# Two feature tiles gated in one operation, the fifth tile's products moved up, and late weight clamps on VectorE

## The chip, the cores and the metric

The kernel runs on one core of a Trainium2 chip. The metric is the device time of one execution in microseconds (us); the kernel before was run three times (median 668.87 us, lowest 668.62, highest 670.48). A further execution was taken with the hardware profiler.

## The reference

Three steps follow one another, in fp32, for a batch of 4 sequences of 768 positions and a width of 384 (8 heads of 48).

```python
# 1. linear attention with a decaying state, per head
for t in range(S):
    cur = einsum('bhd,bhe->bhde', u * k[t], v[t])
    y[t] = einsum('bhd,bhde->bhe', r[t], state + cur)
    state = w * state + einsum('bhd,bhe->bhde', k[t], v[t])
# 2. gated mixer, d_ff = 1024
h = maximum(x @ w_in, 0)
conv = conv_w[0]*h[t-1] + conv_w[1]*h[t] + conv_w[2]*h[t+1]
x = (h * sigmoid(conv)) @ w_out
# 3. second mixer, d_ff = 1536
xn = (x - mean) / sqrt(var + 1e-6) * g_ln
out = x + maximum(xn @ w_ch1, 0) @ w_ch2
```

## The kernel before

**Products in three passes.** A product of fp32 accuracy is made of three TensorE passes: each operand is split into a rounded high part and the rest (names ending in h and l), and high x high, high x low and low x high are added in PSUM. VectorE makes the low part by a subtraction, ScalarE the high part by a copy.

**Attention** works on 24 tiles of 128 positions. Each tile runs as a generator (`attn_tile`, lines 367 to 404; for the first six tiles `light_tile`, lines 318 to 365) in steps: first the element-wise products on VectorE (the decay tables times r and k into `rk`, L373; for the first tiles also `z`, and `kks` by `decayed_k`, lines 252 to 258), then the dot products on TensorE (`dps`) with a masked copy into `aT`, then the products with the values and the state (`yps`), copied out as `xh` and `xl`. A mask selection for each of these tiles runs on POOL (L383, L335). The first four tiles run in `startup()` (lines 434 to 459), between steps of the weight preparation; the fifth is begun by the first step of `attention()` (lines 461 to 483), which then goes on in steps of its own.

**Weights** are prepared in 22 jobs (`wjob`, lines 141 to 174). A job loads a block by DMA from SP's queue, ScalarE takes magnitudes, a clamp follows (`magnitude`, lines 121 to 126), then three integer operations on VectorE, then the high part on ScalarE and the low part on VectorE. The clamp runs on VectorE for jobs 0 to 9 and on POOL for jobs 10 to 21. `wdo(n)` takes n steps of the current job; jobs 0 to 9 belong to the first mixer, jobs 10 to 21 to the second, and of these 15 to 21 are the second half of `w_ch1` and the last four blocks of `w_ch2`. The clamp of a job is issued within the job before it.

**First mixer** (`mixer1`, lines 600 to 614): 8 blocks of 384 positions, 8 feature tiles of 128 in each, 64 feature tiles in all. For each tile `moe1_up` (lines 524 to 539) makes the up-product (nine passes of 386 columns into a PSUM bank, of which there are two), ScalarE makes `h` by relu and the middle tap, VectorE two taps of the convolution (L535). Then `gate` (lines 513 to 516) takes the sigmoid on ScalarE and the product h x gate on VectorE (L516), and `gate_split` (lines 518 to 522) makes high and low part (L521, L522). Both are called for the tile before, while the present one is convolved. `queue_down` puts the tile's down-product (nine passes of 384 columns) into a queue, and `pump(2)` lets all but two of the queue go, so tile f's down-product is issued behind the up-product of tile f + 3. Between tiles, `after1` (lines 834 to 848) takes attention steps: one per tile in the first two blocks, 0.8 later, and weight steps.

**Second mixer** (`mixer2`): 6 blocks of 512 positions, 12 feature tiles each, with relu alone between the up-product and the down-product, queued likewise with `pump(3)`. `prefetch` and `norm` load and normalise the next block's rows meanwhile, with one small power operation per tile on POOL (L572).

**Order.** Operations called through `pe`, `vo`, `ao`, `so` and `go` keep the order in which the program issues them on their engine. Those called through `nc.vector`, `nc.scalar` and `nc.gpsimd` (`v_`, `a_`, `g_`) are placed by a planner when the program is built; `inputs(n)` and `ordered(n)` choose between the two by tile. Helper calls through the ordered engines stand in the profile under line 76.

Of the kernel before, what the change touches and what calls it, by code (L numbers as in the profile page):

```python
# [8 lines left out]
F32 = mybir.dt.float32  # L9
F32R = mybir.dt.float32r  # L10
I32 = mybir.dt.int32
AF = mybir.ActivationFunctionType
ALU = mybir.AluOpType
# [7 lines left out]
NF1 = FF1 // 128  # L21
NF2 = FF2 // 128
C = 128
TPB = S // C
NT = B * TPB
T = 384
TT = T // C
# [8 lines left out]
LAG = 3  # L36
# [13 lines left out]
def body(ctx, tc, r, k, v, w, u, w_in, conv_w, w_out, g_ln, w_ch1, w_ch2, rkT, krv, small, out):  # L50
# [6 lines left out]
    mp = ctx.enter_context(tc.tile_pool(name="mp", bufs=2))  # L57
# [6 lines left out]
    v_ = nc.vector  # L64
# [14 lines left out]
    vo = InOrder(nc.vector)  # L79
    ao = InOrder(nc.scalar)  # L80
    so = InOrder(nc.sync)
    go = InOrder(nc.gpsimd)
# [11 lines left out]
    gl = smallt[:, 3 * NP:]  # L94
# [12 lines left out]
    woh = big.tile([128, NF1, DM], F32R, name="woh")  # L107
    wol = big.tile([128, NF1, DM], F32R, name="wol")
# [12 lines left out]
    def magnitude(st, n, engine=go):  # L121

        t = ap.tile([128, WN], F32, tag="wd", name="wdec", bufs=2)[:, 0:n]
        ao.activation(out=t, in_=words(st, n)[1].bitcast(F32), func=AF.Abs)
        engine.tensor_scalar(out=t, in0=t, scalar1=W_MIN, scalar2=W_MAX, op0=ALU.max, op1=ALU.min)
        return t
# [14 lines left out]
    def wjob(src, n, hi, lo, scale=None):  # L141

        st, mag = [], []

        def load():
            st.append(io.tile([128, 2 * WN], I32, tag="st" if me >= 4 else "first", name="st", bufs=3 if me >= 4 else 4))
            dst = st[0][:, 0:2 * n]
            if len(src.shape) == 3:
                dst = dst.rearrange("p (a n) -> p a n", a=src.shape[1])
            so.dma_start(out=dst, in_=src.bitcast(I32))  # L150

        def ahead():
            if not mag:
                mag.append(magnitude(st[0], n, vo if me < 10 else go))

        def steps():
            ahead()
            t = mag[0]
            yield from decode(st[0], n, t)
            if me + 1 < min(len(wjobs), w_loaded[0]):  # L160
                wjobs[me + 1][2]()
            if len(src.shape) == 3:
                t = t.rearrange("p (a n) -> p a n", a=src.shape[1])
            kw = {} if scale is None else {"scale": gl[:, scale:scale + 1]}
            ao.activation(out=hi, in_=t, func=AF.Copy, **kw)
            yield
            if scale is None:
                vo.tensor_tensor(out=lo, in0=t, in1=hi.bitcast(F32), op=ALU.subtract)
            else:
                vo.scalar_tensor_tensor(out=lo, in0=t, scalar=kw["scale"], in1=hi.bitcast(F32),  # L170
                                        op0=ALU.mult, op1=ALU.subtract)
        me = len(wjobs)
        wjobs.append((load, steps(), ahead))
        return len(wjobs) - 1

# [34 lines left out]
    def wdo(count=1, last=None):  # L210

        for _ in range(count):
            while w_done[0] < (len(wjobs) if last is None else last + 1):
                wload(w_done[0] + 3)
                if next(wjobs[w_done[0]][1], "end") != "end":
                    break
                w_done[0] += 1
# [34 lines left out]
    def decayed_k(n):  # L252

        if n < LIGHT:
            vo.tensor_tensor(out=kks[:, n % 2, 0, :, 0:D], in0=loaded[n][1], in1=tku[:, 0], op=ALU.mult)
            return
        inputs(n).tensor_tensor(out=kks[:, n % 2, :, :, 0:D], in0=loaded[n][1].unsqueeze(1).to_broadcast([128, 2, H, D]), in1=tku,
                         op=ALU.mult)
# [175 lines left out]
    def startup():  # L434

        tiles = {n: attn_tile(n) for n in range(EARLY + 1)}

        def on(n):
            next(tiles[n], None)

        decayed = decayed_k
        on(0), decayed(0), on(0)
        on(1), state_sum(0), state_update(0), decayed(1), on(1), state_sum(1)
        wdo(1)
        on(0), on(2), state_update(1), decayed(2)
        wdo(2)
        on(2), state_sum(2), on(0)
        wdo(1)
        on(1), on(3), state_update(2), decayed(3)
        wdo(2)  # L450
        on(3), state_sum(3), on(1)
        wdo(2)
        on(2), state_update(3)
        wdo(3)
        on(2), on(3)
        wdo(1)
        on(3)
        wdo(4)
        return tiles

    def attention(tiles):

        def go_on(n):
            if 0 <= n < NT:
                next(tiles.setdefault(n, attn_tile(n)), None)

        n = EARLY
        go_on(n)
        decayed_k(n)
        yield  # L470
        load_tile(n + 2)
        decayed_k(n + 1)
        go_on(n)
        yield
        for n in range(EARLY, NT):
            state_sum(n)
            state_update(n)
            go_on(n - 1)
            go_on(n + 1)
            yield  # L480
            go_on(n)
            go_on(n + 1)
            yield
# [18 lines left out]
    def down(acc, gh, gl_, wh, wl, f, nf):  # L502
        for t in range(len(acc)):
            sl = slice(t * 128, t * 128 + 128)
            for q, (a, x) in enumerate(((gh, wh), (gh, wl), (gl_, wh))):
                pe.matmul(acc[t], lhsT=a[:, sl], rhs=x, start=(f == 0 and q == 0),
                          stop=(f == nf - 1 and q == 2))
# [5 lines left out]
    def gate(st):  # L513

        a_.activation(out=st["c"], in_=st["c"], func=AF.Sigmoid)
        v_.tensor_tensor(out=st["c"], in0=st["h"][:, 1:T + 1], in1=st["c"], op=ALU.mult)  # L516

    def gate_split(st):
        st["gh"] = mp.tile([128, T], F32R, tag="gh", name="gh", bufs=LAG + 1)
        st["gl"] = mp.tile([128, T], F32R, tag="gl", name="gl", bufs=LAG + 1)  # L520
        a_.activation(out=st["gh"], in_=st["c"], func=AF.Copy)  # L521
        v_.tensor_tensor(out=st["gl"], in0=st["c"], in1=st["gh"].bitcast(F32), op=ALU.subtract)  # L522

    def moe1_up(x, f, prev):
        ps = ps_m.tile([128, 512], F32, tag="m", name="psm")
        mm3(ps[:, 0:T + 2], [wih[:, kt] for kt in range(KT)], [wil[:, kt] for kt in range(KT)], x[0], x[1], slice(f * 128, f * 128 + 128), slice(0, T + 2))
        if prev is not None:
            gate(prev)
        st = {}
        h = st["h"] = mp.tile([128, T + 2], F32, tag="h", name="h", bufs=3)  # L530
        c = st["c"] = mp.tile([128, T], F32, tag="c", name="c", bufs=3)
        a_.activation(out=h, in_=ps[:, 0:T + 2], func=AF.Relu)
        a_.activation(out=c, in_=h[:, 1:T + 1], func=AF.Copy, scale=cw[:, 1, f:f + 1])  # L533
        for tap, o in ((0, 0), (2, 2)):
            v_.scalar_tensor_tensor(out=c, in0=h[:, o:o + T], scalar=cw[:, tap, f:f + 1], in1=c,  # L535
                                    op0=ALU.mult, op1=ALU.add)
        if prev is not None:
            gate_split(prev)
        return st

    def moe2_up(xn, f, cols):
        ps = ps_m.tile([128, 512], F32, tag="m", name="psm")
# [44 lines left out]
    def pump(n):  # L587
        while len(downq) > n:
            downq.pop(0)()

    def queue_down(st, hold, f, nf, wh, wl, then, tiles=TT):
        def go():
            if f == 0:
                hold.extend(new_acc(tiles))
            down(hold, st["gh"], st["gl"], wh(f), wl(f), f, nf)
            if f == nf - 1:
                then(hold)
        downq.append(go)

    def mixer1(x, then, before=lambda f: None, after=lambda f: None):  # L600
        hold, prev = [], None
        for f in range(NF1):
            before(f)
            st = moe1_up(x, f, prev)
            if prev is not None:
                queue_down(prev, hold, f - 1, NF1, lambda f: woh[:, f, :], lambda f: wol[:, f, :], then)
            prev = st
            after(f)
            pump(LAG - 1)
            after(f)  # L610
        before(NF1)
        gate(prev)
        gate_split(prev)
        queue_down(prev, hold, NF1 - 1, NF1, lambda f: woh[:, f, :], lambda f: wol[:, f, :], then)

    def mixer2(xn, tiles, then, before=lambda f: None, after=lambda f: None):
        hold = []
        for f in range(NF2):
            before(f)
            queue_down(moe2_up(xn, f, tiles * C), hold, f, NF2, lambda f: c2h[f // 2][:, f % 2, :],  # L620
                       lambda f: c2l[f // 2][:, f % 2, :], then, tiles)
            pump(LAG)
            after(f)
# [231 lines left out]
    for j in range(NB2):  # L855
# [11 lines left out]
        x1s, xn = normed.pop(j)  # L867
# [74 lines left out]
```

## Time and profile before

| | |
|---|---|
| median of 3 runs | 668.87 us |
| profiled execution | 670.22 us |
| its span (first to last instruction) | 668.4 us |
| mean granted TensorE clock | 0.973 of full speed |
| first up-product of the first mixer | 39.7 us |
| first up-product of the second mixer | 345.9 us |

Times within the profile are in us from the span's start, and durations of single instructions in us or ns. PE is TensorE, PEld its weight load, DVE VectorE, ACT ScalarE, SP the engine that issues the DMAs. Square brackets at the end of a row hold how long the engine stood idle before the instruction and what ended it; where the engine named there had long been done, it was another. The granted clock is a share of 2.4 GHz. Instructions of one engine overlap, so the time from one start to the next can be shorter than a duration.

### The profile page before, as it was taken

How to read it: one execution, taken by the hardware profiler on the slowest of the kernel's cores; microseconds unless marked ns; L12 is line 12 of the kernel's file. 1: busy time of each engine (PE TensorE's matmuls, PEld its weight loads, DVE VectorE, ACT ScalarE, POOL GpSimd, SP SyncE). 2: the span in 40 equal slices, each digit the busy share in tenths (PEclk: the TensorE clock that was granted, in tenths of full speed). 3: DMA queues.
4: the chain of work that ended last, by engine and by line, in shares of the span. 5: the costliest groups of instructions: out<-in, count | busy, mean ns of one | idle time of the engine just before them, and what ended most of it. 6: DMA issues, size and time to landing. Idle time of an engine off the chain costs nothing.

```text
span 668.4 us, 11712 instructions
## 1 busy us (share of the span) xinstructions
PE 633.3 (95%) x4803; PEld 573.2 (86%) x4803; DVE 437.4 (65%) x793; ACT 261.9 (39%) x514; POOL 122.5 (18%) x126
## 2 busy tenths in 40 slices
PE   9948898999998898999999999999999999999996
PEld 5747888989987897899998789999999899999995
DVE  7979999999999999878777953413422422422211
ACT  3455555465655655566764421211221111221110
POOL 6301621330332214112003620100100100100000
PEclk9876898999999999999999999999999999999999
DMA  8916434435262533102205302002001100200101
GB/s 268 313 49 209 144 106 151 135 100 185 71 215 68 173 114 115 37 1 84 71 13 177 95 0 89 8 0 86 10 0 48 49 0 29 67 0 7 42 0 52
DMA packets 25295, 56.51 MB, mean 85 GB/s; under 512 B 2961, under 2 KB 15378, under 8 KB 25234
## 3 DMA queue, kind: packets, MB, share of 16 engines
q1 hardware_dynamic: 25234, 55.68, 26.2%
q8 instruction: 40, 0.66, 0.4%
q14 instruction: 21, 0.17, 0.1%
HBM read 46.24 MB, written 9.44 MB: 83 GB/s over the span
## 4 chain that ended last, share of the span: by engine, by line
PE 50%; DVE 36%; ACT 4%; issue 4%; DMA 3%; POOL 1%; SPq 0%; DVEq 0%; ACTq 0%
PE acc L76 24%; PE psm L76 24%; DVE c L535 8%; DVE wdec L76 6%; DVE aT L389 3%; DVE c L516 3%; DVE gl L522 3%; DVE rk L373 2%; DMA x1b<-x_dram 1%; DVE rk L76 1%; DVE a L380 1%; DVE xl L398 1%; PE pxt L76 1%; DVE av L378 1%; DMA rk<-in_rkT_dram 1%
## 5 line engine op out<-in xcount | busy, mean ns | idle before, releaser
L549 DVE SCALAR_TENSOR_TENSOR rl<-psm,rh 128x512 fp32r<-128x512 f32 x72 | 49.6, 689 | 135.1 <-ACT rh L548 131.6
L548 ACT ACTIVATE rh<-psm 128x512 fp32r<-128x512 f32 x72 | 43.0, 597 | 196.1 <-PE psm L76 195.9
L76 PE MATMUL acc<-c2l,rh 128*128 128x384 f32 x288 | 97.2, 338 | 0.4 <-DVE c2l L76 0.4
L76 PE MATMUL acc<-c2h,rh 128*128 128x384 f32 x288 | 97.1, 337 | 0.0
L76 PE MATMUL acc<-c2h,rl 128*128 128x384 f32 x288 | 97.1, 337 | 0.0
L535 DVE SCALAR_TENSOR_TENSOR c<-h,tables,c 128x384 f32<-128x384 f32 x128 | 89.9, 704 | 7.0 <-ACT c L533 6.4
L76 PE MATMUL psm<-xnh,c1h 128*128 128x512 f32 x216 | 87.2, 404 | 0.8 <-ACT c1h L76 0.8
L76 PE MATMUL psm<-xnh,c1l 128*128 128x512 f32 x216 | 85.3, 395 | 0.3 <-DVE c1l L76 0.3
L76 PE MATMUL psm<-xnl,c1h 128*128 128x512 f32 x216 | 85.5, 396 | 0.0
L76 PE MATMUL psm<-xh,wih 128*128 128x386 f32 x192 | 71.3, 371 | 13.4 <-DVE xl L76 4.4
L76 PE MATMUL psm<-xl,wih 128*128 128x386 f32 x192 | 67.7, 353 | 0.0
L76 PE MATMUL psm<-xh,wil 128*128 128x386 f32 x192 | 67.7, 352 | 0.0
L76 PE MATMUL acc<-woh,gh 128*128 128x384 f32 x192 | 66.5, 347 | 0.0
L76 PE MATMUL acc<-woh,gl 128*128 128x384 f32 x192 | 65.0, 339 | 0.1
L76 PE MATMUL acc<-wol,gh 128*128 128x384 f32 x192 | 65.0, 339 | 0.0
L76 PEld LDWEIGHTS acc<-c2l,rh 128*128 128x128 f32 x288 | 54.1, 188 | 3.6 <-DVE c2l L76 0.8
L76 PEld LDWEIGHTS acc<-c2h,rh 128*128 128x128 f32 x288 | 54.1, 188 | 3.2
L76 POOL TENSOR_SCALAR wdec<-wdec 128x768 f32<-128x768 f32 (+1 forms) x13 | 40.1, 3085 | 86.4 <-ACT wdec L76 86.4
L76 PEld LDWEIGHTS acc<-c2h,rl 128*128 128x128 f32 x288 | 54.1, 188 | 0.0
L572 POOL TENSOR_TENSOR rs<-rs,nhalf 128x1 f32<-128x1 f32 x24 | 16.4, 691 | 199.4 <-DVE rs L571 198.9
L76 PEld LDWEIGHTS psm<-xh,wih 128*128 128x128 f32 x192 | 38.1, 199 | 17.0 <-ACT woh L76 4.6
L521 ACT ACTIVATE gh<-c 128x384 fp32r<-128x384 f32 x64 | 33.5, 523 | 47.2 <-DVE c L516 46.7
(133 smaller groups left out, 1142.3 us busy)
## 6 DMA issues: line engine op xcount, KB each, us to landing
rk<-in_rkT_dram SPq DMA_DIRECT2D x24, 448.0 KB, 4.4
st<-in_moe_w_ch_dram SPq DMA_DIRECT2D x12, 768.0 KB, 6.0
rv<-in_krv_dram SPq DMA_DIRECT2D x18, 448.0 KB, 4.8
kt<-in_krv_dram SPq DMA_DIRECT2D x24, 192.0 KB, 4.3
x_dram<-x SPq DMA_DIRECT2D x24, 192.0 KB, 2.1
x1b<-x_dram SPq DMA_DIRECT2D x24, 192.0 KB, 3.1
out_dram<-x1b SPq DMA_DIRECT2D x24, 192.0 KB, 1.9
st<-in_moe_w_in_dram SPq DMA_DIRECT2D x6, 512.0 KB, 9.2
```

The lines of the kernel that those rows point to most:

```text
L76: return lambda *args, **kw: tc.keep_in_program_order(op(*args, **kw))
L373: inputs(n).tensor_tensor(out=rk, in0=rk, in1=trk, op=ALU.mult)
L378: v_.tensor_tensor(out=av, in0=kks[:, n % 2, 1, :, 0:D], in1=rt, op=ALU.mult)
L380: v_.tensor_reduce(out=a8.rearrange("x (q p) o -> x q (p o)", q=2), in_=av.rearrange("x (p q) d -> x q p d", q=2), axis=AX.X, op=ALU.add)
L389: v_.copy_predicated(out=aT[:, q], mask=later.bitcast(I32).unsqueeze(1).to_broadcast([128, NP, C]), data=dps[q])
L516: v_.tensor_tensor(out=st["c"], in0=st["h"][:, 1:T + 1], in1=st["c"], op=ALU.mult)
L521: a_.activation(out=st["gh"], in_=st["c"], func=AF.Copy)
L522: v_.tensor_tensor(out=st["gl"], in0=st["c"], in1=st["gh"].bitcast(F32), op=ALU.subtract)
L535: v_.scalar_tensor_tensor(out=c, in0=h[:, o:o + T], scalar=cw[:, tap, f:f + 1], in1=c, op0=ALU.mult, op1=ALU.add)
L548: a_.activation(out=gh[:, 0:cols], in_=ps[:, 0:cols], func=AF.Relu)
L549: v_.scalar_tensor_tensor(out=gl_[:, 0:cols], in0=ps[:, 0:cols], scalar=0.0, in1=gh[:, 0:cols].bitcast(F32), op0=ALU.max, op1=ALU.subtract)
L572: g_.tensor_tensor(out=rs[:, 1:2], in0=rs[:, 0:1], in1=nhalf, op=ALU.pow)
```

## The change

`gate` and `gate_split` take a pair of feature tiles: the buffers `h`, `c`, `gh` and `gl` hold two tiles, the convolution still goes tile by tile, and the sigmoid, the product, the high part and the low part are one operation each of 2 x 384 columns. A pair is gated while the next pair's first tile is convolved, and both of its down-products are queued then. `pump` leaves three of the queue after an even tile and two after an odd one. The buffers `gh` and `gl` number three pairs where there were four tiles. In `startup()` the fifth tile's first step and its `decayed_k` come ahead of the last three weight steps, and the step of `attention()` that held them is gone. The clamps of jobs 15 to 21 run on VectorE.

```diff
--- before.py
+++ after.py
@@ -151,7 +151,7 @@
 
         def ahead():
             if not mag:
-                mag.append(magnitude(st[0], n, vo if me < 10 else go))
+                mag.append(magnitude(st[0], n, vo if me < 10 or me >= 15 else go))
 
         def steps():
             ahead()
@@ -455,7 +455,9 @@
         on(2), on(3)
         wdo(1)
         on(3)
-        wdo(4)
+        wdo(1)
+        on(4), decayed(4)
+        wdo(3)
         return tiles
 
     def attention(tiles):
@@ -465,9 +467,6 @@
                 next(tiles.setdefault(n, attn_tile(n)), None)
 
         n = EARLY
-        go_on(n)
-        decayed_k(n)
-        yield
         load_tile(n + 2)
         decayed_k(n + 1)
         go_on(n)
@@ -513,22 +512,23 @@
     def gate(st):
 
         a_.activation(out=st["c"], in_=st["c"], func=AF.Sigmoid)
-        v_.tensor_tensor(out=st["c"], in0=st["h"][:, 1:T + 1], in1=st["c"], op=ALU.mult)
+        v_.tensor_tensor(out=st["c"], in0=st["h"][:, :, 1:T + 1], in1=st["c"], op=ALU.mult)
 
     def gate_split(st):
-        st["gh"] = mp.tile([128, T], F32R, tag="gh", name="gh", bufs=LAG + 1)
-        st["gl"] = mp.tile([128, T], F32R, tag="gl", name="gl", bufs=LAG + 1)
+        st["gh"] = mp.tile([128, 2, T], F32R, tag="gh", name="gh", bufs=3)
+        st["gl"] = mp.tile([128, 2, T], F32R, tag="gl", name="gl", bufs=3)
         a_.activation(out=st["gh"], in_=st["c"], func=AF.Copy)
         v_.tensor_tensor(out=st["gl"], in0=st["c"], in1=st["gh"].bitcast(F32), op=ALU.subtract)
 
-    def moe1_up(x, f, prev):
+    def moe1_up(x, f, st, prev):
         ps = ps_m.tile([128, 512], F32, tag="m", name="psm")
         mm3(ps[:, 0:T + 2], [wih[:, kt] for kt in range(KT)], [wil[:, kt] for kt in range(KT)], x[0], x[1], slice(f * 128, f * 128 + 128), slice(0, T + 2))
         if prev is not None:
             gate(prev)
-        st = {}
-        h = st["h"] = mp.tile([128, T + 2], F32, tag="h", name="h", bufs=3)
-        c = st["c"] = mp.tile([128, T], F32, tag="c", name="c", bufs=3)
+        if not st:
+            st["h"] = mp.tile([128, 2, T + 2], F32, tag="h", name="h", bufs=3)
+            st["c"] = mp.tile([128, 2, T], F32, tag="c", name="c", bufs=3)
+        h, c = st["h"][:, f % 2], st["c"][:, f % 2]
         a_.activation(out=h, in_=ps[:, 0:T + 2], func=AF.Relu)
         a_.activation(out=c, in_=h[:, 1:T + 1], func=AF.Copy, scale=cw[:, 1, f:f + 1])
         for tap, o in ((0, 0), (2, 2)):
@@ -536,7 +536,6 @@
                                     op0=ALU.mult, op1=ALU.add)
         if prev is not None:
             gate_split(prev)
-        return st
 
     def moe2_up(xn, f, cols):
         ps = ps_m.tile([128, 512], F32, tag="m", name="psm")
@@ -588,36 +587,45 @@
         while len(downq) > n:
             downq.pop(0)()
 
-    def queue_down(st, hold, f, nf, wh, wl, then, tiles=TT):
+    def queue_down(gh, gl_, hold, f, nf, wh, wl, then, tiles=TT):
         def go():
             if f == 0:
                 hold.extend(new_acc(tiles))
-            down(hold, st["gh"], st["gl"], wh(f), wl(f), f, nf)
+            down(hold, gh, gl_, wh(f), wl(f), f, nf)
             if f == nf - 1:
                 then(hold)
         downq.append(go)
 
     def mixer1(x, then, before=lambda f: None, after=lambda f: None):
-        hold, prev = [], None
+        hold, prev, st = [], None, None
+
+        def queue(f):
+            for q in range(2):
+                queue_down(prev["gh"][:, q], prev["gl"][:, q], hold, f + q, NF1, lambda f: woh[:, f, :],
+                           lambda f: wol[:, f, :], then)
+
         for f in range(NF1):
             before(f)
-            st = moe1_up(x, f, prev)
-            if prev is not None:
-                queue_down(prev, hold, f - 1, NF1, lambda f: woh[:, f, :], lambda f: wol[:, f, :], then)
-            prev = st
+            if f % 2 == 0:
+                prev, st = st, {}
+            moe1_up(x, f, st, prev if f % 2 == 0 else None)
+            if f % 2 == 0 and f:
+                queue(f - 2)
             after(f)
-            pump(LAG - 1)
+            pump(4-1 - f % 2)
             after(f)
         before(NF1)
+        prev = st
         gate(prev)
         gate_split(prev)
-        queue_down(prev, hold, NF1 - 1, NF1, lambda f: woh[:, f, :], lambda f: wol[:, f, :], then)
+        queue(NF1 - 2)
 
     def mixer2(xn, tiles, then, before=lambda f: None, after=lambda f: None):
         hold = []
         for f in range(NF2):
             before(f)
-            queue_down(moe2_up(xn, f, tiles * C), hold, f, NF2, lambda f: c2h[f // 2][:, f % 2, :],
+            st = moe2_up(xn, f, tiles * C)
+            queue_down(st["gh"], st["gl"], hold, f, NF2, lambda f: c2h[f // 2][:, f % 2, :],
                        lambda f: c2l[f // 2][:, f % 2, :], then, tiles)
             pump(LAG)
             after(f)
```

## Rows read from the trace of the kernel before

**Rows 1.** Page, first part: busy time of each engine, share of the span, instructions.

```profile
PE 633.3 (95%) x4803; PEld 573.2 (86%) x4803; DVE 437.4 (65%) x793; ACT 261.9 (39%) x514; POOL 122.5 (18%) x126
```

**Rows 2.** Busy time by stretch: us; busy us (instructions) per engine; TensorE clock; DMA.

```profile
39.60:60.00 20.40, 13.15 (x63) 12.23 (x63) 17.38 (x34) 10.45 (x19) 3.35 (x4) 0.58 0.31 93
60.00:94.10 34.10, 30.64 (x330) 28.14 (x328) 34.03 (x51) 20.56 (x40) 15.09 (x6) 0.92 0.58 179
94.10:257.00 162.90, 156.14 (x1732) 143.32 (x1730) 159.98 (x262) 89.95 (x187) 41.73 (x37) 0.99 0.40 127
257.00:291.60 34.60, 31.77 (x326) 29.20 (x319) 30.18 (x53) 18.77 (x41) 6.88 (x7) 1.00 0.22 73
291.60:345.90 54.30, 54.25 (x358) 53.34 (x357) 43.19 (x89) 38.34 (x81) 6.79 (x5) 1.00 0.16 52
360.00:386.00 26.00, 24.51 (x126) 21.26 (x125) 22.50 (x42) 10.92 (x17) 14.39 (x9) 1.00 0.39 129
386.00:660.60 274.60, 274.60 (x1399) 248.34 (x1398) 84.16 (x170) 47.47 (x82) 12.05 (x17) 1.00 0.08 27
```

**Rows 3.** Chain that ended last: shares, then start and length of two late pieces.

```profile
PE 50%; DVE 36%; ACT 4%; issue 4%; DMA 3%; POOL 1%; SPq 0%; DVEq 0%; ACTq 0%
...
321.05 1.56 PE acc L76 x9
322.62 1.59 PE psm L76 x9
```

**Rows 4.** Groups of VectorE, 94 to 257 us: count, busy us, mean ns.

```profile
L535 DVE SCALAR_TENSOR_TENSOR c<-h,tables,c 128x384 f32<-128x384 f32 x65 | 48.2, 743 | 1.3 <-ACT c L533 1.0
L522 DVE TENSOR_TENSOR gl<-c,gh 128x384 fp32r<-128x384 f32 x33 | 19.7, 598 | 0.1
...
L516 DVE TENSOR_TENSOR c<-h,c 128x384 f32<-128x384 f32 x33 | 19.0, 576 | 0.9 <-ACT c L515 0.6
```

**Rows 5.** Timeline of VectorE, 195 to 216 us: start, length, instruction.

```profile
207.66 0.95 DVE L257 TENSOR_TENSOR kks<-kt,tables 128x768 f32<-128x768 f32 x1
208.53 0.55 DVE L516 TENSOR_TENSOR c<-h,c 128x384 f32<-128x384 f32 x1
209.00 0.55 DVE L378 TENSOR_TENSOR av<-kks,rv 128x384 f32<-128x384 f32 x1
...
210.64 1.44 DVE L522 TENSOR_TENSOR gl<-c,gh 128x384 fp32r<-128x384 f32 x1
```

**Rows 6.** Timeline of all engines, 36 to 64 us.

```profile
44.01 0.69 DVE L76 TENSOR_TENSOR wil<-wdec,wih 128x512 fp32r<-128x512 f32 x1 [1.26 <-ACT wih L76]
...
51.19 1.22 DVE L76 TENSOR_TENSOR rk<-rk,tables 112x1024 f32<-112x1024 f32 x1
...
52.51 2.08 PE L76 MATMUL dps<-rk 48*128 48x128 f32 x16 [7.16 <-ACT wih L76]
...
53.32 0.69 DVE L76 TENSOR_TENSOR z<-rk 112x512 f32<-112x512 f32 x1
53.92 0.55 DVE L76 TENSOR_TENSOR kks<-kt,tables 128x384 f32<-128x384 f32 x1
```

**Rows 7.** Clamps: on POOL, 290 to 420 us (min/median/max ns); on VectorE, whole span.

```profile
L76 POOL TENSOR_SCALAR wdec<-wdec x7: 2779/3059/3539, 294.1 to 385.0; 128x768 f32<-128x768 f32 x7
...
L76 DVE TENSOR_SCALAR wdec<-wdec 128x768 f32<-128x768 f32 x4 | 2.7, 665 | 1.3 <-ACT wdec L76 1.3
```

**Rows 8.** Timeline of TensorE, 371 to 380 us.

```profile
372.21 0.50 PE L76 MATMUL psm<-xnh,c1h 128*128 128x512 f32 x1 [0.78 <-ACT c1h L76]
...
373.26 0.50 PE L76 MATMUL psm<-xnh,c1l 128*128 128x512 f32 x1 [0.33 <-DVE c1l L76]
...
378.87 0.44 PE L76 MATMUL acc<-c2l,rh 128*128 128x384 f32 x1 [0.38 <-DVE c2l L76]
```

**Rows 9.** Timeline of POOL, one mask selection.

```profile
210.33 1.35 POOL L383 TENSOR_SCALAR_AFFINE_SELECT aT<-a 128x1024 f32<-128x1024 f32 x1 [8.15 <-DVE a L380]
```

**Rows 10.** Timeline of TensorE, 262 to 266 us.

```profile
264.31 0.44 PE L76 MATMUL psm<-xh,wih 128*128 128x386 f32 x1 [2.38 <-DVE xl L398]
```

## The prediction

> **What bounds the kernel now.** I began with the page's first part [rows 1]: TensorE is busy for 95% of the span, VectorE for 65%. That average hides two stages, so the next view was busy time by stretch [rows 2]. From 60 to 257 us VectorE has no free time (34.03 of 34.10 us, then 159.98 of 162.90), while TensorE leaves 3.46 and 6.76 us. From 291.6 us on TensorE is full (54.25 of 54.30, at the end 274.60 of 274.60) and VectorE has room (43.19 of 54.30, later 84.16 of 274.60). In the first stretch, 39.6 to 60 us, neither is full: VectorE has 3.02 us free, and TensorE stands idle for a third of it and runs at a granted clock of 0.58. In 360 to 386 us TensorE loses 1.49 us again. The chain of waits agrees [rows 3]: half of it is TensorE, 36% VectorE, and in the late stage it runs from nine down-products (1.56 us) to nine up-products (1.59 us) and back without a gap. So the kernel is first a sum of VectorE work, up to the end of attention, and then a sum of TensorE work. A saving on VectorE counts only in the first part; work that is pushed from the first part into the second is paid on TensorE.
>
> The profiled execution took 670.22 us for a span of 668.4. The three runs shown have a median of 668.87, so it lies 1.35 us above it, inside their spread. The terms below are differences; I take them off the median.
>
> **Part 1, gating two feature tiles at once.** Per pair, two products (L516) and two subtractions (L522) of 384 columns become one each of 768, on VectorE; on ScalarE two sigmoids and two copies likewise become one each. What VectorE saves depends on how a saved instruction counts. Their durations are 576 and 598 ns [rows 4]; a two-input operation of 768 columns takes 0.95 us [rows 5]. By durations a pair saves 2 x 0.576 - 0.95 + 2 x 0.598 - 0.95 = 0.45 us. But instructions overlap: in [rows 5] the 768-column one at 207.66 is followed by L516 at 208.53 and that by the next at 209.00, so in a full queue they cost 0.87 and 0.47 us, and a pair saves 2 x (0.94 - 0.87) = 0.14 us. VectorE's queue is full where the saving counts, so I take 0.14. Attention ends with about 46 of the 64 feature tiles done, hence 23 pairs: -3.2 us. Bounds: -10.3 (23 x 0.45) and 0 (the freed time becomes idle time). The new access pattern, two rows of 384 with a step, costs nothing extra as far as rows go: the 0.95 us operation also walks more than one dimension.
>
> The Trainium skill, page "VectorE: DVE Perf Modes", section "The TRN2 errata — SBUF-src ops pay a fixed extra latency per instruction", gives fp32 two-tensor operations as (N + 151) / 0.96 ns, a fixed part of 157 ns. The durations of 0.55 and 0.95 us agree with that. By it 46 saved instructions would give an estimated 7.2 us in place of 3.2, and the sum would be 660.9; the start-to-start times in [rows 5] speak for less than half of that.
>
> On ScalarE the pair's operations save time too, but it is busy for 89.95 of 162.90 us in the VectorE stage [rows 2]: nothing, and its cover would have to shrink by nearly half before it counted.
>
> The change also adds a wait: the sigmoid of an even tile now waits for the odd tile's convolution. Behind it on ScalarE stand the next relu copies, for which TensorE waits when both up-product banks are full. The sigmoid of the last tile already waited for that same convolution; it is the first half that is delayed, so I cost the wait at nothing. Every down-product comes one place later in TensorE's order (part 2), so the pair's first tile has as much cover as before and its second tile one up-product and one down-product more.
>
> **Part 2, down-products one place later.** The queue now holds tile 0's down-product until tile 4 has been multiplied, where it was tile 3. Until VectorE stops being the bound that hides in TensorE's free time; at the switch one more down-product is left for the stage in which TensorE is full, 1.56 us [rows 3]. Bounds 0 (if TensorE has the time at the switch) and 1.56; I take it whole, since [rows 2] shows 54.25 of 54.30 there.
>
> **Part 3, the fifth tile moved up.** Its three operations, rk 1.22, z 0.69 and kks 0.55 us, now run at 51 to 54 us [rows 6]; the change puts them about 41 us, ahead of the last three weight steps of the start-up. Their DMAs were issued long before, with the tables. VectorE's work stays the same; what can shrink is its idle time of 3.02 us. Its largest piece is the 1.26 us before wil at 44.01 [rows 6], a wait for a ScalarE copy: 2.46 us of tile work ahead of it should cover that. TensorE's 7.16 us gap before the dot products at 52.51 should go as well, but there VectorE sets the pace. Against it, the 16 dot products (2.08 us) and the 8 small ones that follow now stand ahead of the second up-product, so its convolution comes later. I take -1.5 us, the 1.26 and a little of the rest; bounds -3.0 and +1.5 (2.08 and about as much again, less the 2.46 us that cover it).
>
> All later attention steps come one step earlier, with their loads: the seventh tile's three transfers pass one weight load on SP's queue, which is fetched two jobs ahead, at no cost; on POOL the mask selections only come earlier. At 0.8 step per feature tile, attention ends 1.25 tiles sooner, and so 1.25 tiles more lie in the TensorE stage. Each costs 3.15 us there [rows 3] and takes 2 x 0.743 + 0.576 + 0.598 = 2.66 us out of the VectorE stage [rows 4]: 1.25 x 0.49 = +0.6 us.
>
> **Part 4, late clamps on VectorE.** Jobs 15 to 21 leave POOL: seven of 3.06 us (median) from 294 us on, against 665 ns on VectorE [rows 7]. VectorE has 3.50 us free in 360 to 386 us [rows 2] and gets 3.3 to 4.7 us in all from 294 to 390, so that is hidden; if it were not, the free time's shortfall, about 1 us, would be paid. Each weight's serial chain becomes 2.4 us shorter, and TensorE's waits for weights are 0.78, 0.33 and 0.38 us [rows 8], together the 1.49 us of [rows 2]. They should go: -1.5 us; bounds -1.5 and +1.0.
>
> **Sum.** -3.2 + 1.56 - 1.5 + 0.6 - 1.5 = -4.0 us: 664.9 us.
>
> **Rivals.**
> (a) Durations count, not starts: where VectorE's results are waited for in turn (ScalarE waits for L516 and L522's neighbours), the whole latency of a saved operation goes. Then part 1 is -10.3 and the time 657.8. For it: a VectorE operation behind POOL's mask selection is stretched to 1.44 us [rows 5], its partner being the selection at 210.33 [rows 9], and fewer operations meet fewer of those. Against it: the starts.
> (b) The saving doesn't reach the end: TensorE takes its products in order and at feature tile borders waits for attention (2.38 us for xl at 264.31 [rows 10]); if that wait, not VectorE's sum, sets the pace, part 1 gives nothing and VectorE merely idles. -0.7 us: 668.2.
> (c) Slower: the longer operation stands in front of xl or the masked products. A 768-column product ahead of them takes 0.95 us where it was 0.55, and TensorE waits in order. With 0.40 us more at each of the 18 tiles after the start-up ones that is 7.2 us, and the sum turns to +3.2: 672.1. It decides once VectorE has nothing else to do in that wait, that is, from idle time on VectorE of more than about 4 us beyond the 2.92 of 94.1 to 257 us [rows 2]. For it: waits like [rows 10]. Against it: VectorE is full there, so work does not run out. The Trainium skill, "Perfetto Trace Analysis", section "Optimizing Scalar/DVE Operations", speaks that way: where VectorE isn't saturated but causes bubbles elsewhere, breaking instructions up may finish work sooner. This trace has it saturated up to 257 us.
>
> **How the numbers follow.** Likeliest case 0.53, with its own range of 661 to 668; (a) 0.15, (b) 0.18, (c) 0.14. The range of 659 to 670.5 takes in the bounds of parts 3 and 4 and case (b), and leaves out the far end of (a) and most of (c), some 0.2. A measurement here can tell about 0.3% (2.0 us) from no change, so faster means under 666.9 and slower over 670.9. Faster: most of the likeliest case (0.45), (a) and a little of (b): 0.64. Slower: most of (c) and a bit of the likeliest case's upper end: 0.14. Same: 0.22.
>
> **What would show it.** Right: L516 and L522 with half the instructions at about 0.95 us; VectorE still full from 60 us to the end of attention, and that end 4 to 6 us sooner; TensorE's gap near 45 to 52 us mostly gone; POOL without clamps after about 260 us and no TensorE waits for c1h, c1l, c2l. Wrong: VectorE with clear idle time between 94 and 257 us (b, c), longer TensorE waits for xl or aT (c), a second up-product so late that the first stretch is not shorter (part 3), or new waits at the rl operations of 360 to 386 us (part 4).

## The result and the profile after

**Time.** 675.67 us, the median of 4 runs (674.13 to 676.2), against 669.23 for the kernel before beside it (4 runs): a ratio of 1.009, 95% interval 1.0067 to 1.0113. Slower, where I forecast 664.9, and outside the range. The profiled execution has a span of 674.1 us; before it was 668.4.

The profile page's busy line and its chain:

```profile
PE 634.4 (94%) x4803; PEld 575.8 (85%) x4803; DVE 434.1 (64%) x736; ACT 253.8 (38%) x450; POOL 88.5 (13%) x119
...
PE 62%; DVE 25%; issue 3%; ACT 3%; DMA 1%; POOL 0%; DVEq 0%; ACTq 0%
```

Against [rows 1] VectorE has 57 instructions less and 3.3 us less work, POOL 34 us less, TensorE the same number of products. The chain has moved from VectorE (36% in [rows 3], now 25%) to TensorE (50%, now 62%): the stage that TensorE bounds has grown. Busy time by stretch, columns as in [rows 2]:

```profile
39.60:60.00 20.40, 17.81 (x153) 15.81 (x153) 17.60 (x36) 11.78 (x22) 2.29 (x4) 0.67 0.43 133
60.00:94.10 34.10, 21.27 (x187) 19.84 (x191) 28.58 (x39) 15.28 (x27) 10.37 (x6) 0.71 0.50 155
94.10:257.00 162.90, 154.57 (x1702) 141.19 (x1694) 158.93 (x230) 84.84 (x157) 35.14 (x35) 1.00 0.41 127
...
291.60:345.90 54.30, 54.30 (x359) 53.70 (x358) 40.88 (x71) 35.41 (x61) 3.77 (x4) 1.00 0.16 52
...
360.00:386.00 26.00, 26.00 (x135) 23.48 (x134) 24.27 (x51) 12.55 (x19) 3.37 (x4) 1.00 0.51 172
```

The second stretch stands out: from 60 to 94.1 us TensorE does 187 instructions where it did 330, and VectorE, which had no free time there, has 5.5 us. In the last row TensorE is full from 360 to 386 us, so the waits that part 4 was after are gone. TensorE's timeline from 55 to 98 us, the rows with a wait and the up-product behind the longest one, says what stops TensorE:

```profile
60.55 0.69 PE L76 MATMUL psm<-xh,wih 128*128 128x386 f32 x1 [1.83 <-ACT aT L334]
...
83.11 2.08 PE L76 MATMUL dps<-rk 48*128 48x128 f32 x16 [12.28 <-DVE rk L76]
85.12 0.69 PE L76 MATMUL psm<-xh,wih 128*128 128x386 f32 x1
...
95.43 1.16 PE L76 MATMUL dps<-rk 48*128 48x128 f32 x16 [1.02 <-ACT h L532]
```

TensorE stands still for 12.28 us, called the hole from here on, until the product `rk` of the seventh tile is there. The up-product at 85.12 is the sixth. In the kernel before, the sixth up-product came ahead of the same dot products, which had no wait:

```profile
76.41 0.34 PE L76 MATMUL psm<-xh,wih 128*128 128x386 f32 x1
...
82.22 1.16 PE L76 MATMUL dps<-rk 48*128 48x128 f32 x16
```

VectorE's timeline of the hole and what follows it, in the changed kernel:

```profile
76.34 0.95 DVE L76 TENSOR_TENSOR kks<-kt,tables 128x768 f32<-128x768 f32 x1
77.21 0.95 DVE L76 TENSOR_TENSOR wol<-wdec,woh 128x768 fp32r<-128x768 f32 x1
...
79.48 0.95 DVE L76 SCALAR_TENSOR_TENSOR wdec<-st,wdec 128x768 int32<-128x768 int32 x1
...
80.81 1.11 DVE L76 SCALAR_TENSOR_TENSOR wdec<-st,wdec 128x768 int32<-128x768 int32 x1
81.84 1.21 DVE L76 TENSOR_TENSOR rk<-rk,tables 112x1024 f32<-112x1024 f32 x1
82.98 0.95 DVE L76 TENSOR_TENSOR wol<-wdec,woh 128x768 fp32r<-128x768 f32 x1
85.29 1.34 DVE L389 COPY_PREDICATED aT<-tables,dps 128x512 f32<-128x512 int32 x2 [1.37 <-PE dps L76]
89.64 1.23 DVE L373 TENSOR_TENSOR rk<-rk,tables 112x1024 f32<-112x1024 f32 x1 [3.01 <-DMA rk<-in_rkT_dram]
...
92.97 0.96 DVE L515 TENSOR_TENSOR c<-h,c 128x768 f32<-128x768 f32 x1 [0.91 <-ACT c L514]
```

That `rk` stands behind all but the last of the first mixer's weight steps. When they are done VectorE itself runs dry: the next convolutions belong to up-products that stand behind the dot products in TensorE's order. From the first up-product to the ninth it is idle for 8.4 us; before it was 3.1. Before, the same `rk` came ahead of the last weight job's steps, in VectorE's timeline of the kernel before:

```profile
74.31 1.23 DVE L76 TENSOR_TENSOR rk<-rk,tables 112x1024 f32<-112x1024 f32 x1
75.44 0.96 DVE L76 SCALAR_TENSOR_TENSOR wdec<-st,wdec 128x768 int32<-128x768 int32 x1
...
81.60 0.95 DVE L76 TENSOR_TENSOR wol<-wdec,woh 128x768 fp32r<-128x768 f32 x1
```

The chain that ended last, the kernel after, 40 to 120 us (start, length, piece), adds the load that comes next:

```profile
79.56 0.87 DVE wdec L76
80.89 1.03 DVE wdec L76
81.92 1.15 DVE rk L76
83.11 2.13 PE dps L76 x16
85.26 4.29 DMA rk<-in_rkT_dram
89.64 1.23 DVE rk L373
```

SP issues this load at 85.26, just when the late dot products have ended, and VectorE waits for it: 3.01 us of its idle time.

**The end of attention.** The last `xl` of attention, in the kernel before and then after (VectorE's L398 from 285 to 310 us: min/median/max ns, first and last start):

```profile
L398 DVE TENSOR_TENSOR xl<-yps,xh x2: 554/555/556, 287.5 to 297.7; 128x384 fp32r<-128x384 f32 x2
```

```profile
L398 DVE TENSOR_TENSOR xl<-yps,xh x2: 553/556/558, 287.2 to 298.3; 128x384 fp32r<-128x384 f32 x2
```

Attention ends no sooner, at 298.8 us with the operation's length against 298.3. The prediction's signs named an end 4 to 6 us sooner, and its own terms add up to 8.0 us. But fewer feature tiles are done by then: in the trace 14.0 up-products and 17.9 down-products follow it before, 16.0 and 20.1 after. From there TensorE is full, so all of it is paid. The table cuts each profiled execution at the first up-product, at the ninth (slot 8), the 41st (slot 40), the end of the last `xl`, and the first up-product of the second mixer. Its last columns hold VectorE's idle time in the three stretches from the first up-product to the last `xl`, and its busy time in all three:

```
kernel     first up  slot 8  slot 40  last xl  mixer 2  span  | mixer 2 - xl  to end | VectorE idle to slot 8, to 40, to xl | busy
before         39.7    94.1    252.1    298.3    345.9  668.4 |         47.6   322.5 |  3.1  2.9  5.5 | 247.2
after          40.3   100.5    259.9    298.8    351.4  674.1 |         52.6   322.7 |  8.4  3.9  6.2 | 240.1
```

### The profile page after: what moved, and what is told of

Read it like the earlier page. It is cut to its first block, busy times and chain, and to the rows that moved or that the text cites. A ratio compares the mean times of both kernels' runs of the same rounds, so it can differ in the third digit from the quotient of the medians.

```text
span 674.1 us, 11573 instructions
## 1 busy us (share of the span) xinstructions
PE 634.4 (94%) x4803; PEld 575.8 (85%) x4803; DVE 434.1 (64%) x736; ACT 253.8 (38%) x450; POOL 88.5 (13%) x119
## 4 chain that ended last, share of the span: by engine, by line
PE 62%; DVE 25%; issue 3%; ACT 3%; DMA 1%; POOL 0%; DVEq 0%; ACTq 0%
PE psm L76 30%; PE acc L76 29%; DVE c L535 7%; DVE wdec L76 3%; DVE aT L389 3%; DVE rk L373 2%; DVE gl L521 2%; DVE c L515 2%; PE yps L76 2%; DMA rk<-in_rkT_dram 1%; PE pxt L76 1%; ACT c L514 1%; DVE a L380 1%; DVE av L378 1%; DVE kks L257 1%
## 5 line engine op out<-in xcount | busy, mean ns | idle before, releaser
L76 PEld LDWEIGHTS psm<-xnh,c1l 128*128 128x128 f32 x216 | 40.5, 188 | 9.5
L532 ACT ACTIVATE h<-psm 128x386 f32<-128x386 f32 x64 | 31.2, 488 | 44.2 <-PE psm L76 43.7
```

What stands on the lines that cost most here:

```text
L76: return lambda *args, **kw: tc.keep_in_program_order(op(*args, **kw))
```

## The experiments

All are given as edits of the kernel before or after, with the ratio to the kernel before beside them. Each kernel has one profile, and single numbers of the table at the end of this section are read to about 1 us: the first up-product, which stands ahead of most of what the edits touch, lies between 39.0 and 41.0 us in it.

**First set: each part alone, and the change without part 3.** 668.57 us for the kernel before.

Late clamps alone (before):

```
-    mag.append(magnitude(st[0], n, vo if me < 10 else go))
+    mag.append(magnitude(st[0], n, vo if me < 10 or me >= 15 else go))
```

> The kernel before with the late clamps on VectorE alone. If they do what the prediction said, TensorE's 1.49 us of waits in the second mixer's first half block go and the time falls by 1 to 2 us (ratio 0.997 to 0.9985). If the waits are only replaced by others, no change (0.999 to 1.001).

The move alone (before):

```
-        wdo(4)
+        wdo(1)
+        on(4), decayed(4)
+        wdo(3)
...
-        go_on(n)
-        decayed_k(n)
-        yield
```

> The kernel before with the fifth tile's products moved up alone. Theory A (the earlier attention steps put the seventh tile's rk product behind the last weight steps on VectorE while TensorE's order has its dot products ahead of the next up-product): a TensorE gap of 8 to 13 us between 65 and 90 us, and a ratio of 1.006 to 1.012. Theory B (the pairs are the cause): no such gap, ratio 0.995 to 1.000.

The pairs alone, with their later down-products: the change without the two edits above.

> The kernel before with the gating in pairs alone (down-products one place later). Theory A: ratio 0.995 to 1.001, the start-up as before. Theory B: most of the loss is here, ratio 1.005 to 1.010, with VectorE idle in the first block while the pair waits for its second tile.

The change without the move:

> The changed kernel without the moved-up tile: pairs and late clamps. Theory A: ratio 0.993 to 0.999, and the gap between 65 and 90 us gone. Theory B: 1.003 to 1.008.

Measured: clamps 666.28, ratio 0.9954 [0.9933, 0.9975]; the move **675.61, 1.0093 [1.0059, 1.0127]**; pairs 666.8, 0.9965 [0.9945, 0.9985]; pairs and clamps without the move 666.47, 0.995 [0.9927, 0.9972]. The move by itself costs what the whole change costs. The clamps gain more than the 1 to 2 us expected. TensorE's waits, first of the kernel with the move alone, then of the change without it:

```profile
PE dps L76 <- DVE rk L76: 17.0, 3, 14.7
```

```profile
PE dps L76 <- ACT wih L76: 6.9, 1, 6.9
```

With the move the wait for `rk` is there without pairs and without clamps; without the move it is not, and the older gap of [rows 6] stays. The pairs and the clamps are gains, but they do not add up: both remove the second mixer's waits for weights [rows 8], the pairs by leaving one more down-product to be multiplied ahead of them.

**Second set: which piece of the move, and is the hole the cause?** 669.59 us for the kernel before.

The fifth tile moved up in the start-up, all later attention steps left where they were (after):

```
         n = EARLY
+        yield
         load_tile(n + 2)
```

> The changed kernel with an empty first attention step, so that the fifth tile's first products are moved up but no later step comes earlier. If the earlier later steps are what costs (theory A), the gap between 65 and 90 us goes and the ratio is 0.992 to 0.998. If moving the fifth tile's products ahead of the weight steps costs by itself (theory C: weights late, or the second up-product late), the ratio stays at 1.003 to 1.009.

Down-products one place earlier (after):

```
-            pump(4-1 - f % 2)
+            pump(2 - f % 2)
```

> The changed kernel with the down-products one place earlier (two of the queue left after an even tile, one after an odd one), as in the kernel before. If the later down-products feed the gap (TensorE has one less of them before the seventh tile's dot products) and cost 1.56 us at the switch, the time falls by 1.5 to 4 us against the changed kernel (ratio 1.003 to 1.007). If they cost nothing: 1.008 to 1.010; if the pair then comes late, longer waits for gl and more than 1.010.

The seventh tile's `rk` placed by the planner, so that it need not stand behind the weight steps (after):

```
-        inputs(n).tensor_tensor(out=rk, in0=rk, in1=trk, op=ALU.mult)
+        (nc.vector if n == 6 else inputs(n)).tensor_tensor(out=rk, in0=rk, in1=trk, op=ALU.mult)
```

> The changed kernel with one edit: the seventh tile's rk product alone no longer keeps the program's order on VectorE. Theory A with its place in VectorE's queue as the cause: the product runs before 75 us, the 12.28 us gap of TensorE shrinks to under 4 us and the time falls by 4 to 8 us (ratio 0.997 to 1.003). If the gap is only a symptom of VectorE's total work: the gap moves to another place and the ratio stays at 1.006 to 1.010.

Three weight steps per feature tile of the first block, where there were four (after):

```
-                wdo(2, wo_job[NF1 - 1])
+                wdo(1 + slot[0] % 2, wo_job[NF1 - 1])
```

> The changed kernel with three weight steps per feature tile in the first block where there were four, so that the rk product of the seventh tile stands ahead of one weight job more on VectorE. Theory A: gap halved or better, ratio 1.000 to 1.006. If the weights were what the first block waits for: no gain, ratio 1.008 or more.

Measured: without the shift 669.14, 0.9988 [0.9959, 1.0016]; earlier down-products 682.19, 1.0182 [1.0134, 1.023]; free `rk` 675.57, 1.0083 [1.0056, 1.011]; slower weights 671.48, 1.0028 [1.0007, 1.0048].

The shift of the steps is most of the loss: it makes the difference between 0.9988 and 1.009. That 0.9988 lies between the two cases set down, so it leaves open whether the moved first products cost something too. The free `rk` contradicts the simple form of my theory, that this one product's place in VectorE's queue makes the hole. VectorE's row, and TensorE's last wait of the block, in that kernel:

```profile
52.33 1.22 DVE L373 TENSOR_TENSOR rk<-rk,tables 112x1024 f32<-112x1024 f32 x1 [3.44 <-DMA rk<-in_rkT_dram]
```

```profile
89.41 1.09 PE L76 MATMUL pst<-rv,kks 128*64 128x48 f32 x16 [13.04 <-issue]
```

```profile
88.60 1.33 DVE L389 COPY_PREDICATED aT<-tables,dps 128x512 f32<-128x512 int32 x2
```

`rk` runs at 52 us and a hole is there all the same, 13.04 us, one step of the tile further on: its `aT` copies, VectorE's row at 88.60, stand behind the weight steps just as `rk` did. The profile names no releaser for that wait; that it ends with the first of the two copies is my reading. VectorE's idle time in the block stays at 8.4 us, but 3.44 of them are new, the wait for this `rk`'s own load in the row at 52.33. So the run shows that this one operation isn't enough, and not what a free `rk` with its data in time would give. Slower weights let VectorE reach the tile sooner, and the wait shrinks:

```profile
75.62 2.08 PE L76 MATMUL dps<-rk 48*128 48x128 f32 x16 [7.04 <-DVE rk L76]
```

VectorE's idle time in the block falls to 3.2 us and the time by 0.6%, with the shift kept. It does not fall to that of the kernel before. The earlier down-products I had wrong: I thought them a cheap 1.5 us, but the pairs need the cover, as TensorE's waits in that kernel show:

```profile
PE acc L76 <- DVE gl L521: 13.7, 12, 2.5
```

VectorE's idle time between slots 8 and 40 is 12.5 us there against 3.9.

**Third set: hole or lead?** 669.9 us for the kernel before. The shift does two things: it puts the seventh tile early (the hole), and it keeps attention a step ahead to the end (the lead). An empty step in the loop gives the lead back at one point (after, with 5 and with 8):

```
         for n in range(EARLY, NT):
+            if n == 5:
+                yield
```

> The changed kernel with an empty attention step ahead of the step that starts the seventh tile: the fifth and sixth tile stay early, the seventh and all later ones stand where they stood before. If the early seventh tile is the cause (TensorE's order has its dot products before the sixth up-product), the 12 us gap goes and the ratio is 0.994 to 1.000. If the cause is the earlier fifth and sixth tile, 1.005 to 1.009.

> The changed kernel with the empty step only ahead of the step that starts the tenth tile (three tiles later). If the early seventh tile is the cause: the gap between 65 and 90 us stays, ratio 1.006 to 1.011. If the cause is that attention ends sooner and leaves more work to TensorE's stage, the loss goes: 0.997 to 1.003.

And the slower weights without the shift, on the change without the move and on the clamps alone, to see whether slower weights are a gain by themselves:

> Pairs and late clamps without the moved tile, and three weight steps per feature tile in the first block where there were four. If VectorE's order in the first block still costs there, another 1 to 3 us: ratio 0.990 to 0.994. If VectorE's sum sets the pace, no change against pairs and clamps: 0.994 to 0.997.

> The kernel before with the late clamps on VectorE and three weight steps per feature tile in the first block. The same two cases: 0.990 to 0.994, or as the clamps alone, 0.994 to 0.998.

Measured: back from the seventh tile 668.56, 0.9979 [0.9959, 0.9998]; from the tenth 670.28, 1.0002 [0.9981, 1.0023]; slower weights 666.89, 0.9956 [0.9938, 0.9975], and 667.39, 0.9952 [0.9932, 0.9971]. TensorE's wait for the seventh tile, first with the lead given back there, then from the tenth on:

```profile
77.71 2.08 PE L76 MATMUL dps<-rk 48*128 48x128 f32 x16 [3.39 <-DVE rk L76]
```

```profile
82.61 2.08 PE L76 MATMUL dps<-rk 48*128 48x128 f32 x16 [13.67 <-DVE rk L76]
```

The second of them is the surprise: the hole is as large as in the changed kernel, and yet the time is that of the kernel before. So a hole with the lead given back costs little (0.2%, and the two intervals overlap), and keeping the lead costs 0.9% more. Slower weights gain nothing where there is no hole (0.9956 against 0.995, 0.9952 against 0.9954): they help only where the move is.

```
kernel             first up  slot 8  slot 40  last xl  mixer 2  span  | mixer 2 - xl  to end | VectorE idle to slot 8, to 40, to xl | busy
clamps alone           39.4    93.8    251.8    297.5    344.9  663.3 |         47.4   318.4 |  3.1  2.6  5.5 | 247.0
the same, slower w.    39.5    94.6    252.6    298.5    345.8  663.9 |         47.4   318.1 |  3.4  2.7  5.5 | 247.4
pairs alone            40.4    95.3    249.8    297.6    344.6  666.1 |         47.0   321.5 |  2.5  4.1  7.6 | 243.0
pairs and clamps       39.3    94.4    249.3    296.4    344.0  665.1 |         47.6   321.1 |  2.7  4.4  7.1 | 243.0
the same, slower w.    39.0    95.3    249.9    295.5    343.2  664.3 |         47.7   321.1 |  4.1  4.1  5.6 | 242.7
move alone             40.6   102.3    264.2    303.4    355.0  673.4 |         51.6   318.4 |  8.1  5.4  5.1 | 244.2
no shift               41.0    96.9    251.7    298.8    346.5  667.7 |         47.7   321.2 |  5.9  4.5  7.0 | 240.5
lead back at 7th       40.6    95.4    251.7    298.8    346.5  667.0 |         47.7   320.5 |  4.8  5.8  7.0 | 240.6
lead back at 10th      40.1   100.0    254.6    300.2    347.9  668.4 |         47.7   320.5 |  8.3  5.1  5.6 | 241.0
after                  40.3   100.5    259.9    298.8    351.4  674.1 |         52.6   322.7 |  8.4  3.9  6.2 | 240.1
after, slower w.       39.0    96.4    255.4    294.2    346.8  668.7 |         52.6   321.9 |  3.2  4.0  6.1 | 241.9
```

The column "mixer 2 - xl" separates the two: in this table it is 51.6 to 52.6 us wherever the lead is kept, and 47.0 to 47.7 wherever it is not. The lead costs TensorE's stage 4 to 5 us. It should be earned back by less work for VectorE up to the last `xl`, and so by an earlier last `xl`. VectorE's columns, with the lead less without it, show what became of that:

```
with the lead    without it                    work left out   busy   idle   last xl
move alone       before                                  2.7   -3.0   +7.1      +5.1
after            pairs and clamps                        3.9   -2.9   +4.3      +2.4
after            no shift                                3.9   -0.4   +1.1       0.0
after, slower w. pairs and clamps, slower w.             3.9   -0.8   -0.5      -1.3
```

"Work left out" is the four or five operations that the kernel with the lead leaves for after the last `xl` (two taps, the product and the subtraction, with the pairs a clamp), at their mean durations. Where the hole and the early first tiles come together, idle time eats the gain. In the last row VectorE is no emptier with the lead than without it, and even there attention ends only 1.3 us sooner, with a ratio of 1.0028 against 0.9956. There it is the work that hardly shrinks: other operations have become longer, the taps of the convolution most of all. From the first up-product to the last `xl`, slower weights with and then without the move:

```profile
L535 DVE SCALAR_TENSOR_TENSOR c<-h,tables,c 128x384 f32<-128x384 f32 x96 | 70.0, 733 | 4.4 <-ACT c L533 3.4
```

```profile
L536 DVE SCALAR_TENSOR_TENSOR c<-h,tables,c 128x384 f32<-128x384 f32 x98 | 67.7, 692 | 6.3 <-ACT c L534 5.5
```

Without pairs they take 732 ns before and with the move alone. Why they are shorter in pairs, and not when the lead is kept, no run shows.

## Why the prediction was wrong

The forecast split into the same pieces: attention's end by -3.2 (part 1), -3.3 (the lead, 1.25 x 2.66) and -1.5 us (start-up), together -8.0 (the signs in the prediction say 4 to 6, which doesn't follow from these terms); the lead's tiles on TensorE +3.9 (1.25 x 3.15); the rest +1.56 - 1.5, near zero. Measured in the spans: attention's end +0.5, then +5.0, then +0.2. So 8.5 of the 9.7 us that I missed lie ahead of attention's end. Rival (b)'s sum is a slip as well: without part 1 it is -0.8 us and 668.1, not -0.7 and 668.2.

**Part 3 is the step that failed**, in its second paragraph: "All later attention steps come one step earlier", set down as an even exchange between two full stages, "1.25 x 0.49 = +0.6 us". Measured, the shift alone (after against no shift) is 6.4 us of span, 1.009 against 0.9988. The cost on TensorE came, and larger: two up-products and one down-product more are left at the last `xl`, 4.9 us in the table where I had 3.9, and 1.5 us more behind. The gain on VectorE, 3.3 us, did not come: attention ends at 298.8 us in both.

Two things took the gain, in shares that differ with the pair compared. One is the hole, a wait that the prediction didn't have at all, since I had added up VectorE's work without laying TensorE's order against VectorE's in the first block. The step that moved brings the seventh tile's dot products ahead of the sixth up-product, while its products on VectorE fall behind the weight steps; TensorE stands still for 12.28 us, and VectorE's idle time up to slot 8 is 5.3 us longer than before. The other is that VectorE's work ahead of the switch shrank by less than what was left out of it, in the two pairs of the table whose idle time differs least by 0.4 and 0.8 us in place of some 3.9. Two ways to divide the whole loss come out alike. With the lead given back from the tenth tile the hole and the moved start-up cost 0.5% (1.0002 against 0.995 for pairs and clamps), and keeping the lead costs 0.9% more. With slower weights, which leave VectorE no emptier than without the move, the move still costs 0.7% (1.0028 against 0.9956), of 1.4% otherwise. The move alone measured +0.93%, some 6 us, where I had -0.9 (-1.5 + 0.6).

**The start-up's -1.5 us did not come.** Rows of after, and the second up-product of the kernel before:

```profile
41.45 1.22 DVE L76 TENSOR_TENSOR rk<-rk,tables 112x1024 f32<-112x1024 f32 x1
...
44.14 2.08 PE L76 MATMUL dps<-rk 48*128 48x128 f32 x16 [0.63 <-ACT h L532]
...
45.89 0.69 DVE L76 TENSOR_TENSOR wil<-wdec,wih 128x512 fp32r<-128x512 f32 x1 [0.36 <-ACT wih L76]
...
47.88 0.67 PE L76 MATMUL psm<-xh,wih 128*128 128x386 f32 x1
...
48.44 0.80 DVE L76 TENSOR_SCALAR wdec<-wdec 128x24 int32<-128x24 int32 x1 [1.52 <-POOL wdec L76]
```

```profile
42.73 0.53 PE L76 MATMUL psm<-xh,wih 128*128 128x386 f32 x1
```

The wait for `wih` fell from 1.26 to 0.36 us as forecast, but the one for POOL's small clamp grew from 0.34 to 1.52, and the second up-product comes at 47.88, where it came at 42.73. In the kernel without the shift, which has this part of the move alone on top of pairs and clamps, the last `xl` comes 2.4 us later than without it, and VectorE's idle time to slot 8 is 5.9 us against 2.7. But 1.7 of the 2.4 us stand already at the first up-product, and the intervals of the two ratios (0.9988 and 0.995) overlap: the gain is not there, and a loss is likely but not shown. I had named the later second up-product and bounded its cost at +1.5.

**Part 1 was right in size only between slots 8 and 40.** L515 and L521, VectorE from 94 to 257 us:

```profile
L521 DVE TENSOR_TENSOR gl<-c,gh 128x768 fp32r<-128x768 f32 x16 | 16.1, 1004 | 0.0
...
L515 DVE TENSOR_TENSOR c<-h,c 128x768 f32<-128x768 f32 x16 | 15.2, 951 | 1.9 <-ACT c L514 1.8
```

Half the instructions at 0.95 to 1.00 us, as said. With clamps alone slots 8 to 40 take 158.0 us, with the pairs added 154.9: 3.1 us for 16 pairs, 0.19 a pair, where I took 0.14 from the starts and the durations gave 0.45. That weighs the Trainium skill's rule too: "VectorE: DVE Perf Modes", section "The TRN2 errata — SBUF-src ops pay a fixed extra latency per instruction", would have two saved operations return 157 ns each, an estimated 0.31 a pair. The durations agree with it; the saving is less, since starts overlap. But at attention's end only 1.1 us of it is left (297.5 to 296.4; 3.0 with slower weights on both sides): up to there VectorE is busy for 4.0 us less and idle for 3.0 us more. Its taps wait longer for ScalarE's middle tap, as VectorE's waits from the first up-product to the last `xl` show, clamps alone and then pairs and clamps:

```profile
DVE c L535 <- ACT c L533: 3.1, 5, 1.0
```

```profile
DVE c L536 <- ACT c L534: 6.6, 7, 2.3
```

I had put the added wait of the pair on ScalarE at nothing; that it is the reason is not shown. After attention's end the pairs cost some 2.7 us: nine products more after the second mixer's start (1.56, **part 2**, as priced), and TensorE's wait of 0.34 us for the longer `gl`:

```profile
359.61 0.45 PE L76 MATMUL acc<-woh,gl 128*128 128x384 f32 x1 [0.34 <-DVE gl L521]
```

So on top of the clamps the pairs change nothing that can be told, and rival (b), a saving that does not reach the end, was closer than I held it. Alone they gain 0.35%; in the profiles 1.3 us of it lie ahead of the second mixer and 1.0 behind its start, where the waits of [rows 8] are gone. Part 2 was needed besides: in the changed kernel the time rises by about 1% without it (1.0182 against 1.009).

**Part 4 was right in kind and too small for the clamps alone.** 0.46% (3.1 us) against 1.5; on top of the pairs it adds nothing that can be told (0.995 against 0.9965). Its row of 360 to 386 us, clamps alone:

```profile
360.00:386.00 26.00, 25.94 (x136) 23.18 (x135) 25.71 (x49) 13.12 (x19) 3.50 (x4) 1.00 0.30 96
```

TensorE's waits, 1.49 us in [rows 2], are gone; in the two profiles the stage from the second mixer's start on is 4.1 us shorter (322.5 to 318.4). I had counted the waits alone. The products themselves also took less time, which was not in that sum: before, the 1600 from there on have 314.8 us of busy time, with the clamps 311.7. Why is not shown.

**The rivals.** (a) did not occur. (c) ended on the right side, but its mechanism, a longer operation ahead of `xl`, is not what happened: the change without the move has those operations and is faster. None of the three held the seventh tile's wait or a lead that VectorE doesn't pay back, and nothing in the range stood for either.

**Best version.** The change without part 3, or the late clamps alone: 0.995 [0.9927, 0.9972] and 0.9954 [0.9933, 0.9975], both faster than either kernel.

**Open.** Why VectorE's taps are longer with the lead than without it. Also, after the second mixer's start the changed kernel's profile is 1.5 to 2.2 us longer than those without the lead and with the same products (322.7 against 320.5 to 321.2); no run was aimed at either.

## What to carry to other kernels

When a step of an in-order schedule is moved, lay the orders of all engines that it touches side by side: what stands behind it on the engine that waits, and what stands ahead of its inputs on the engine that feeds it. Getting one part ahead is an exchange only if the bound engine has that much less to do before the switch, in busy and in idle time together; here it had not, and the displaced products were paid whole in the next stage. And a wait does not go with the one operation that ends it: with the free `rk` a hole of the same size stood one step of the tile further on.

## What was not expected of the hardware

The hole costs TensorE its clock. Busy time and granted clock of the changed kernel in the hole, in the dot products right behind it, and in those of the next tile:

```profile
70.90:83.10 12.20, 0.00 (x0) 0.00 (x0) 12.20 (x18) 4.63 (x6) 3.91 (x2) 0.59 0.73 229
83.11:85.20 2.09, 2.09 (x17) 1.87 (x17) 0.82 (x1) 0.00 (x0) 2.09 (x2) 0.50 0.00 0
95.43:96.60 1.17, 1.17 (x17) 1.05 (x17) 1.17 (x2) 0.99 (x2) 0.00 (x0) 1.00 0.88 193
```

After 12 us without a product the clock stands at the lower of its two levels (0.50, 1.2 GHz), and the same sixteen products take 2.08 us; at the upper level (1.00, 2.4 GHz) they take 1.16. The first row also shows that VectorE was full through the whole hole: its idle time comes behind it, while TensorE catches up.
